# Folding the even channels twice in a Fourier-mixing kernel

## The chip, the cores and the metric

The kernel runs as one program on one core of a Trainium2 chip. The time is device microseconds (us) of an execution; lower is better. Six executions of the kernel before were timed, and one of them was profiled.

## The reference

Two blocks follow each other, all in float32. The first is attention that keeps, for each query, its 32 largest scores; its result, with the heads laid side by side, is `x` of shape (8, 576, 512). The second is a Fourier mixing block with an MLP:

```python
X = np.fft.fft(x, axis=1)          # over 576 tokens
X = np.fft.fft(X, axis=2)          # over 512 channels
u = x + np.real(X)
un = (u - mean(u)) / sqrt(var(u) + 1e-6)
out = u + np.maximum(un @ w_ch1, 0.0) @ w_ch2     # 512 -> 2048 -> 512
```

The change touches only the two Fourier transforms, which are done as matrix products with tables of cosines and sines.

## The kernel before

**Batches and steps.** There are 8 batches of 36 steps (4 pairs of heads by 9 tiles of queries). In each step TensorE computes scores (`sp`, line 360) and transposes an earlier tile's weights (`tpP`, L427), VectorE finds the 32 largest scores with four `MAX8` and three `MATCH_REPLACE8` (L381, L383), GpSimd turns them into bounds (`nt`, L390), ScalarE and GpSimd mask the scores with those bounds (L397, then L400), and ScalarE takes the exponential (L406). When a batch's attention is over, its Fourier transforms come within the first 16 or so steps of the next batch, and its MLP (`hp` L832, `cp` L859, `cw` and `cv` L1029) is cut into units that fill TensorE's free time in the steps that follow. A planner (`plan`, `costs`, `level`, the loop from L1348) assigns every piece to a step at build time from estimated costs. The emitted order is the order in which each engine executes; nothing is reordered at run time between the queues. The planner's estimate for the channel transform is 1.75 us a tile and for the token transform 4.3 us per parity (L1291, L1295).

**The folds.** A transform of real data by cosines and sines needs half the products if entries that mirror each other are added or subtracted first. For each parity `par` of the output token, `fold_ops` (L582) makes four operations: `first` adds or subtracts the two halves of the tokens (`sd`, L602), `second` adds and subtracts the two halves of the channels (`zw`, L565), giving 256 columns for the even output channels and 256 for the odd ones, and two calls of `fold_channels` (L546) fold each of these 256 once more about its middle (`fg`, L549). `fold_tails` does the same for the 64 left-over tokens into `ftail`. The fold operations run on GpSimd for batches 1 to 6, one operation to a step there (batch 1: the last two in one step), and on VectorE for batches 0 and 7, all in a row. On GpSimd they stand in a step behind that step's masking (L400) and ahead of its bounds (L390), so the next step's masking waits for them.

**The token transform.** `half_of_tokens` (L620) takes 128 folded channels as the stationary operand and a table `fs` of 145 columns as the moving one, for three blocks of tokens. Half `g2` = 0 holds the even channels (cosine part and sine part), `g2` = 1 the odd ones. One middle channel of the even half is computed by three products with one stationary column each. ScalarE writes the result `yp` to `y`, twice: as it is, and mirrored (L658 to L660), the mirrored sine part through a multiplication with a sign from `sg`.

**The channel transform.** `dft_channels` (L669) multiplies, for each of a batch's five token tiles, four blocks of `y` (128 channels each) with the table `fd`: two blocks make the 256 even output channels, two the 256 odd ones. Its result `mp` is copied to `us` by ScalarE, interleaved so that even and odd channels alternate (L699), and GpSimd adds it to `x` (L705); in batches 0 and 7 VectorE adds it to `x` directly (L688). Mean and variance (L710), the transpose `tpu` (L747) and the MLP follow.

A float32 product appears in the trace as two passes, so 15 products of the token transform for one parity show as 30 matmul records, and the channel transform of one tile as 8. A transpose is one record.

Of the kernel before, what the change touches and what calls it, by code (L numbers as in the profile page):

```python
# [9 lines left out]
F32 = mybir.dt.float32  # L10
# [3 lines left out]
ALU = mybir.AluOpType  # L14
# [4 lines left out]
P = 128  # L19
# [3 lines left out]
def _tables(S, DM):  # L23

    kq = S // 4 + 1
    p = np.arange(P)
    fs = np.zeros((P, 2, 2, 3, kq), dtype=np.float64)
    for par in range(2):
        kk = 2 * np.arange(kq) + par
        for st in range(3):
            tok = P * st + p
            if st == 2:  # L40

                tok = np.where(p < TH, tok, S // 2 + tok - TH)
            a = 2.0 * np.pi * ((np.outer(tok, kk) % S) / S)
            fs[:, 0, par, st] = np.cos(a)
            fs[:, 1, par, st] = np.sin(a)
    d = np.arange(DM // 4)
    m = np.arange(DM // 2)

    def ang(dd, ll):
        return 2.0 * np.pi * ((np.outer(dd, ll) % DM) / DM)  # L50

    se = -np.sin(ang(d, 2 * m))
    se[0] = np.cos(np.pi * m)
    so = -np.sin(ang(d + 1, 2 * m + 1))
    fd = np.stack([np.cos(ang(d, 2 * m)), se, np.cos(ang(d, 2 * m + 1)), so], axis=1)
    sg = -np.ones((P, 2))
    sg[0, 0] = 1.0
    return (
        fs.astype(np.float32), fd.astype(np.float32), sg.astype(np.float32),
        np.eye(P, dtype=np.float32),  # L60
    )
# [3 lines left out]
def kernel(  # L65
# [9 lines left out]
    nc = tc.nc  # L75
    B, H, S, D = q.shape
    DM = H * D
    DF = moe_w_ch1.shape[1]
    scale = 1.0 / float(D) ** 0.5
    HS = S // 2  # L80
    NC = 5
    NF = NC - 1
    TAIL = 2 * TH
# [44 lines left out]

    ident = const.tile([P, P], F32, name="ident", tag="ident")
    fs = const.tile([P, 2, 2, 3, KQ], F32, name="fs", tag="fs")  # L130
    fd = const.tile([P, 4, DM // 2], F32, name="fd", tag="fd")
    sg = const.tile([P, 2], F32, name="sg", tag="sg")
    w1 = const.tile([P, NDT, DF], F32, name="w1", tag="w1")
    w2 = const.tile([P, NIT, DM], F32, name="w2", tag="w2")
    mv = [const.tile([P, 5, 2], F32, name=f"mv{i}", tag=f"mv{i}") for i in range(2)]
# [401 lines left out]
        return 0.14 * len(CHUNKS[ch])  # L537


    def two(ap):  # L540
        return ap.rearrange("p (m two) -> p two m", two=2)

    Q1, Q2, Q3 = DM // 4, DM // 2, 3 * DM // 4
    folded, y_of, yt_of, us_of, rs_of, unT_of = ({} for _ in range(6))

    def fold_channels(eng, z, f, n):  # L546

        def tt(out, up, down, op):
            eng.tensor_tensor(out=f[..., out], in0=z[..., up], in1=z[..., down], op=op)  # L549

        if n == 0:
            eng.memset(f[..., Q1:Q1 + 1], 0.0)
            eng.tensor_copy(out=f[..., 0:DM:Q2], in_=z[..., 0:DM:Q2])
            up, down = slice(1, Q1), slice(Q2 - 1, Q1, -1)
            tt(up, up, down, ALU.add)
            tt(slice(Q1 + 1, Q2), up, down, ALU.subtract)
        else:
            up, down = slice(Q2 + 1, Q3), slice(DM - 1, Q3, -1)
            tt(up, up, down, ALU.subtract)
            tt(slice(Q3, DM - 1), up, down, ALU.add)  # L560
            eng.tensor_copy(out=f[..., DM - 1:DM], in_=z[..., Q3:Q3 + 1])

    def fold_halves(eng, s_, z):
# [3 lines left out]
    def fold_tails(b, eng):  # L567


        f, got = ftail[0:TAIL], []  # L570

        def first():
            got.append(batp.tile([P, DM], F32, name=f"zt_{b}", tag="fold_s")[0:TAIL])
            fold_halves(eng, x_of[b][0:TAIL, 4, :], got[0])

        def third():
            fold_channels(eng, got[0], f[:, 0:DM], 1)
            eng.tensor_copy(out=f[:, DM:DM + 1], in_=got[0][:, Q1:Q1 + 1])

        return [first, lambda: fold_channels(eng, got[0], f[:, 0:DM], 0), third]  # L580

    def fold_ops(b, par, eng, space="own"):  # L582

        x = x_of[b]

        if space == "hT":
            sp = batp.tile([P, NIT * CW[0]], F32, name=f"fsp_{b}", tag="hT")

        def buf(n, name):
            if space == "hT":
                return sp[:, 2 * DM * n:2 * DM * (n + 1)].rearrange("p (s c) -> p s c", s=2)
            pool, tag = (batp, ("fold_s", "fold_d")) if space == "own" else (attp, ("PT0", "PT1"))
            return pool.tile([P, 2, DM], F32, name=f"{name}_{b}_{par}", tag=tag[n % 2], bufs=1)

        got = folded[b, par] = []

        def first():
            got.append(buf(0, "sd"))  # L600
            op = ALU.add if par == 0 else ALU.subtract
            eng.tensor_tensor(out=got[0], in0=x[:, 0:2, :], in1=x[:, 2:4, :], op=op)  # L602

        def second():
            got.append(buf(1, "zw"))
            fold_halves(eng, got[0], got[1])

        def third(n):
            if n == 0:
                got.append(buf(2, "fg"))  # L610
            fold_channels(eng, got[1], got[2], n)

        return [first, second, lambda: third(0), lambda: third(1)]

    def dft_tokens(b, par):
        for g2 in range(2):
# [3 lines left out]
    def half_of_tokens(b, par, g2):  # L620
# [11 lines left out]
        def mm(gg, st, lhsT, rows, table, start=False):  # L632

            nc.tensor.matmul(  # L634
                yp[0:rows, gg, :],
                lhsT=lhsT,
                rhs=fs[:, table, par, st, :],
                start=start,
                stop=st == 2,
                skip_group_check=True,  # L640
            )


        for gg in range(2):
            g = 2 * g2 + gg
            for st in range(3):
                f = fg[:, st] if st < 2 else ftail
                mm(gg, st, f[:, P * g:P * (g + 1)], P, gg, start=gg == 0 and st == 0)
        if g2 == 0:
            for st in range(3):  # L650
                mm(1, st, zw[:, st, Q1:Q1 + 1] if st < 2 else ftail[:, DM:DM + 1], 1, 0)

        mir, back = (
            (slice(HS + 2, S, 2), slice(KQ - 2, 0, -1)) if par == 0
# [1 line left out]
        )  # L656
        y2 = y[:, 2 * g2:2 * g2 + 2, :]
        nc.scalar.copy(out=y2[:, :, par:HS + 1:2], in_=yp[:, :, 0:KQ - par])  # L658
        nc.scalar.copy(out=y2[:, 0, mir], in_=yp[:, 0, back])
        nc.scalar.mul(out=y2[:, 1, mir], in_=yp[:, 1, back], mul=sg[:, g2:g2 + 1])  # L660
        if par == 1 and g2 == 1:
            tails_of_y(b)

# [5 lines left out]
    def dft_channels(b, t, quick=False):  # L669

        rows, y = ROWS[t], y_of[b]
        shape, name = [P, 2, DM // 2], f"mp_{b}_{t}"
        mp = ps_s.tile(shape, F32, name=name, tag="sp") if b == B - 1 else bank(shape, name)
        for par in range(2):
            for j in range(2):
                g = 2 * par + j
                if t == 4:
                    lhsT = yt_of[b][:, g].rearrange("p h r -> p (h r)")
                else:
                    k0 = HS * (t // 2) + P * (t % 2)  # L680
                    lhsT = y[:, g, k0:k0 + P]
                nc.tensor.matmul(  # L682
                    mp[0:rows, par, :], lhsT=lhsT, rhs=fd[:, g, :],
                    start=(j == 0), stop=(j == 1),
                )
        if quick:
            xt = two(x_of[b][0:rows, t, :])
            at(now[0], "dve", lambda: nc.vector.tensor_tensor(  # L688
                out=xt, in0=mp[0:rows], in1=xt, op=ALU.add
            ))  # L690
# [5 lines left out]
                [P, 2 if key[1] else 3, DM], F32, name=f"us_{b}_{t}", tag="fold_d" if key[1] else "fold_s"  # L696
            )
        us = us_of[key][0:rows, CHUNKS[int(key[1])].index(t), :]
        nc.scalar.copy(out=two(us), in_=mp[0:rows])  # L699
        return 1.75  # L700

    def add_mixed(b, t):
# [802 lines left out]
```

## Time and profile before

| what | value |
|---|---|
| median of 6 runs | 1911.79 us (1910.22 to 1912.96) |
| the profiled execution's own time | 1912.96 us |
| its span, first to last instruction | 1911.2 us |
| TensorE busy | 1796.9 us (94%) |
| VectorE busy | 1583.4 us (83%) |
| ScalarE busy | 1210.3 us (63%) |
| GpSimd busy | 877.2 us (46%) |
| mean granted TensorE clock | 0.974 |
| chain of waits: share on TensorE | 81% |

The engines are named PE (TensorE), PEld (its weight loads), DVE (VectorE), ACT (ScalarE), POOL (GpSimd) and SP (the queue that issues most transfers). The chain of waits follows the work that ended last back from the end: at each step to what released it, or to the instruction before it on its engine. "x8" behind a chain piece counts matmul records. In the lists in order of time, the first number is the start in us and the second the duration of the merged piece; an arrow in brackets names what ended the idle time before it.

### The profile page before, as it was taken

The numbers are of one execution on the slowest core, as the hardware profiler recorded it, in microseconds if no ns is written. First come the engines' busy times: TensorE is split into PE (matmuls) and PEld (weight loads), VectorE is DVE, ScalarE is ACT, GpSimd is POOL, SyncE is SP. The second block draws the span as 40 slices with busy tenths as digits, with TensorE's granted clock in tenths as the row PEclk, the third lists the DMA queues.
The fourth block names the chain that finished last, engine by engine and source line by source line (L and its number), as shares of the span: only waits on it lengthen the run. The fifth ranks groups of instructions, "written<-read, shape, count | busy, mean of one in ns | idle before, by whom it ended". The sixth has DMA issues, their size and how long they took to land.

```text
span 1911.2 us, 28279 instructions
## 1 busy us (share of the span) xinstructions
PE 1796.9 (94%) x9008; PEld 1190.8 (62%) x9008; DVE 1583.4 (83%) x3277; ACT 1210.3 (63%) x3078; POOL 877.2 (46%) x1158
## 2 busy tenths in 40 slices
PE   5567799999999999999999999999999999999999
PEld 3344465474666756766567656667567656667677
DVE  7999989999999999989898898888899888862110
ACT  6878657676766767666676667766676667652100
POOL 4768643555635454345535454355535454341012
PEclk7787899999999999999999999999999999999999
DMA  5333002211104111140013101140013102030132
GB/s 167 103 95 107 20 13 61 88 56 25 47 24 119 31 27 41 42 121 19 19 47 110 46 14 52 42 121 19 19 47 101 52 17 59 23 102 6 50 106 73
DMA packets 184339, 111.34 MB, mean 58 GB/s; under 512 B 125952, under 2 KB 174208, under 8 KB 184192
## 3 DMA queue, kind: packets, MB, share of 16 engines
q1 hardware_dynamic: 183408, 109.33, 20.2%
q8 instruction: 72, 1.18, 0.3%
q14 instruction: 75, 0.61, 0.1%
q10 hardware_dynamic: 784, 0.21, 0.0%
HBM read 93.76 MB, written 15.73 MB: 57 GB/s over the span
## 4 chain that ended last, share of the span: by engine, by line
PE 81%; ACT 7%; DVE 6%; POOL 3%; DMA 2%; issue 1%; SPq 0%; POOLq 0%; DVEq 0%; ACTq 0%
PE hp L832 25%; PE cp L859 11%; PE o L464 8%; PE tpP L427 6%; PE sp L360 6%; PE cw L1029 5%; PE cv L1029 4%; PE yp L634 3%; PE mp L682 3%; PE cp L898 3%; DVE m L381 3%; DVE wk L383 2%; PE sp_t L330 2%; POOL wk L400 1%; ACT wk L406 1%
## 5 line engine op out<-in xcount | busy, mean ns | idle before, releaser
L400 POOL TENSOR_TENSOR wk<-S,wk 128x576 f32<-128x576 f32 x288 | 408.3, 1418 | 771.0 <-ACT wk L397 742.4
L381 DVE MAX8 m<-wk 128x8 f32<-128x576 f32 x864 | 626.5, 749 | 6.1
L832 PE MATMUL hp<-unT,w 128*128 128x256 f32 (+1 forms) x2048 | 538.4, 410 | 2.6 <-ACT unT L750 2.6
L832 PEld LDWEIGHTS hp<-unT,w 128*128 128x128 f32 x2048 | 373.7, 191 | 124.2 <-issue 25.0
L383 DVE MATCH_REPLACE8 wk<-m,wk 128x576 f32<-128x576 f32 x576 | 427.6, 742 | 0.0
L406 ACT ACTIVATE wk<-wk,nt 128x576 f32<-128x576 f32 x288 | 224.9, 781 | 71.6 <-POOL wk L400 67.5
L427 PE MATMUL tpP<-ident,wk 128*128 128x128 f32 x1152 | 183.1, 283 | 70.8 <-ACT wk L406 43.1
L430 ACT COPY PT<-tpP 128x512 f32<-128x512 f32 (+1 forms) x320 | 171.4, 547 | 111.9 <-PE tpP L427 109.6
L859 PE MATMUL cp<-w,hT 128*128 128x512 f32 x512 | 240.6, 598 | 0.0
L397 ACT ACTIVATE wk<-S,nt 128x576 f32<-128x576 f32 x288 | 226.9, 788 | 19.4 <-POOL nt L390 18.4
L427 PEld LDWEIGHTS tpP<-ident,wk 128*128 128x128 f32 x1152 | 140.7, 145 | 143.6 <-ACT wk L406 66.2
L836 ACT ACTIVATE hT<-hp 128x320 f32<-128x320 f32 (+1 forms) x256 | 104.9, 410 | 193.6 <-PE hp L832 191.5
L381 DVE MAX8 m<-S 128x8 f32<-128x576 f32 x288 | 213.8, 743 | 5.3 <-ACT S L334 5.3
L383 DVE MATCH_REPLACE8 wk<-m,S 128x576 f32<-128x576 f32 x288 | 213.7, 742 | 0.0
L464 PE MATMUL o<-PT,v 128*64 128x256 f32 (+3 forms) x1440 | 193.4, 411 | 1.7 <-ACT PT L430 1.7
L363 ACT COPY S<-sp 128x512 f32<-128x512 f32 (+1 forms) x264 | 141.9, 589 | 51.7 <-PE sp L360 51.5
L360 PE MATMUL sp<-kT,qT 64*128 64x512 f32 (+1 forms) x528 | 159.0, 661 | 4.3 <-ACT means L1217 3.3
L464 PEld LDWEIGHTS o<-PT,v 128*64 128x64 f32 x1440 | 110.5, 151 | 73.1 <-issue 15.7
L859 PEld LDWEIGHTS cp<-w,hT 128*128 128x128 f32 x512 | 88.8, 190 | 86.3 <-issue 86.2
L974 POOL TENSOR_TENSOR hT<-hT 128x512 f32<-128x512 f32 x64 | 81.5, 1276 | 101.0 <-ACT hT L836 89.3
L1029 PE MATMUL cw<-w,hT 128*128 128x256 f32 x448 | 106.8, 383 | 2.7 <-DMA w<-w_parts 1.3
L1029 PEld LDWEIGHTS cw<-w,hT 128*128 128x128 f32 x448 | 81.4, 190 | 20.4 <-issue 6.4
(143 smaller groups left out, 2149.0 us busy)
## 6 DMA issues: line engine op xcount, KB each, us to landing
w<-w_parts SPq DMA_DIRECT2D x82, 512.0 KB, 4.4
space<-in_moe_w_ch_dram SPq DMA_DIRECT2D x32, 512.0 KB, 3.6
nat<-in_q_dram SPq DMA_DIRECT2D x128, 64.0 KB, 2.3
v<-in_v_dram SPq DMA_DIRECT2D x128, 64.0 KB, 2.2
out_dram<-x SPq DMA_DIRECT2D x32, 256.0 KB, 2.1
nat<-in_k_dram SPq DMA_DIRECT2D x124, 64.0 KB, 2.2
w_parts<-w_t SPq DMA_DIRECT2D x8, 512.0 KB, 2.9
w_s<-w_parts SPq DMA_DIRECT2D x8, 512.0 KB, 5.0
```

Of the source, the lines that this page charges most:

```text
L360: nc.tensor.matmul(sp[r], lhsT=qT[hd, q_cols], rhs=kT[hd, :], start=True, stop=True)
L381: ops.append(lambda src=src, m8=m8: nc.vector.max(out=m8, in_=src))
L383: ops.append(lambda src=src, m8=m8: nc.vector.match_replace(w, m8, src, NEG))
L397: nc.scalar.activation(out=w, in_=Ssb[i], func=AF.Relu, scale=-FAR, bias=Nt[i][:, 1:2])
L400: nc.gpsimd.tensor_tensor(out=w, in0=Ssb.pop(i), in1=w, op=ALU.subtract)
L406: nc.scalar.activation(out=w, in_=w, func=AF.Exp, bias=Nt.pop(i)[:, 0:1], accum_out=den_t[pair % 3][:, c:c + 1],)
L427: nc.tensor.transpose(tp[:, c, :], p_sb[:, k0 + P * c:k0 + P * (c + 1)], ident)
L430: nc.scalar.copy(out=pt[:, NF * he:NF * (he + 1), col:col + w], in_=tp[:, :, o:o + w])
L464: nc.tensor.matmul(o[D * e:D * (e + 1), c0:c1], lhsT=vv[:, c, e, :], rhs=pt[:, 2 * NF if c == NF else NF * e + c, c0:c1], start=(c == 0), ...
L832: nc.tensor.matmul(hp[:, 0:w], lhsT=w1[:, dt, P * it:P * (it + 1)], rhs=unT[:, dt, 0:w], start=(dt == 0), stop=(dt == NDT - 1),)
L859: nc.tensor.matmul(cp, lhsT=hT[:, it, P * n:P * (n + 1)], rhs=w2[:, it, :], start=(it == 0), stop=(it == NIT - 1),)
L1029: nc.tensor.matmul(dst, lhsT=h()[a][:, kc, :], rhs=rhs_of(kc), start=start and kc == 0, stop=kc == NK - 1, skip_group_check=True,)
```

## The change

The even half of the channels is folded once more. After the first fold of the 256 even columns into 128 sums and 128 differences (now kept in 256 extra columns `c` behind `fg`), each of these 128 is folded about its own middle into 64 cosine and 64 sine columns. `fold_channels` now has three parts: part 0 the first even fold (into `c`), part 1 the second even fold (four additions or subtractions of 63 or 64 columns, one zeroed column, one copied column), part 2 the odd fold with one more copied column. In `fold_ops` parts 0 and 1 form the third operation of the four, part 2 the fourth; in `fold_tails` part 0 joins the first operation, part 1 is the second, part 2 the third.

In the token transform the even half's two groups of 128 channels now each hold 64 cosine and 64 sine columns. Each is done as two products with 64 stationary columns, one into result rows 0 to 63 with the cosine table and one into rows 64 to 127 with the sine table, alternating: 12 products in place of 6 per parity. The three products with one column remain, with row 64 of the first group as their result. The mirrored copy of the first even group becomes a multiplication by a sign (64 rows of each), where it was a plain copy.

In the channel transform the even half becomes two independent products of 128 moving columns, one for the output channels that are a multiple of four and one for those two beyond, in place of two accumulated products of 256 columns. The odd half keeps its two products of 256 columns, with its table's columns in another order. The result now holds four groups of 128, and `us` and the addition to `x` interleave with a step of four elements in place of two.

The costs and steps in the planner stay as they were.

```diff
-    def fold_channels(eng, z, f, n):
+    def fold_channels(eng, z, f, c, n):
         if n == 0:
-            eng.memset(f[..., Q1:Q1 + 1], 0.0)
-            eng.tensor_copy(out=f[..., 0:DM:Q2], in_=z[..., 0:DM:Q2])
+            eng.tensor_copy(out=c[..., 0:Q1 + 1:Q1], in_=z[..., 0:Q1 + 1:Q1])
             up, down = slice(1, Q1), slice(Q2 - 1, Q1, -1)
-            tt(up, up, down, ALU.add)
-            tt(slice(Q1 + 1, Q2), up, down, ALU.subtract)
+            tt(c, up, z, up, down, ALU.add)
+            tt(c, slice(Q1 + 1, Q2), z, up, down, ALU.subtract)
+        elif n == 1:
+            up, down = slice(0, Q0), slice(Q1, Q0, -1)
+            tt(f, slice(0, Q0), c, up, down, ALU.add)
+            tt(f, slice(Q1, Q1 + Q0), c, up, down, ALU.subtract)
+            up, down = slice(Q1 + 1, Q1 + Q0), slice(Q2 - 1, Q1 + Q0, -1)
+            tt(f, slice(Q0 + 1, Q1), c, up, down, ALU.subtract)
+            tt(f, slice(Q1 + Q0 + 1, Q2), c, up, down, ALU.add)
+            eng.memset(f[..., Q0:Q0 + 1], 0.0)
+            eng.tensor_copy(out=f[..., Q1 + Q0:Q1 + Q0 + 1], in_=c[..., Q1 + Q0:Q1 + Q0 + 1])
         else:
...
+            eng.tensor_copy(out=f[..., Q2:Q2 + 1], in_=z[..., Q2:Q2 + 1])
             eng.tensor_copy(out=f[..., DM - 1:DM], in_=z[..., Q3:Q3 + 1])
...
-        return [first, second, lambda: third(0), lambda: third(1)]
+        def both():
+            third(0)
+            third(1)
+
+        return [first, second, both, lambda: third(2)]
...
                 f = fg[:, st] if st < 2 else ftail
-                mm(gg, st, f[:, P * g:P * (g + 1)], P, gg, start=gg == 0 and st == 0)
+                first = gg == 0 and st == 0
+                if g2:
+                    mm(gg, st, f[:, P * g:P * (g + 1)], slice(0, P), gg, first)
+                    continue
+                for h in range(2):
+                    c0 = P * g + P // 2 * h
+                    mm(gg, st, f[:, c0:c0 + P // 2], slice(P // 2 * h, P // 2 * (h + 1)), h, first)
         if g2 == 0:
             for st in range(3):
-                mm(1, st, zw[:, st, Q1:Q1 + 1] if st < 2 else ftail[:, DM:DM + 1], 1, 0)
+                f, c = (fg[:, st], DM + Q0) if st < 2 else (ftail, DM)
+                mm(0, st, f[:, c:c + 1], slice(Q0, Q0 + 1), 0)
...
-        nc.scalar.copy(out=y2[:, 0, mir], in_=yp[:, 0, back])
-        nc.scalar.mul(out=y2[:, 1, mir], in_=yp[:, 1, back], mul=sg[:, g2:g2 + 1])
+        if g2:
+            nc.scalar.copy(out=y2[:, 0, mir], in_=yp[:, 0, back])
+        else:
+            nc.scalar.mul(out=y2[:, 0, mir], in_=yp[:, 0, back], mul=sg[:, 0:1])
+        nc.scalar.mul(out=y2[:, 1, mir], in_=yp[:, 1, back], mul=sg[:, 1 + g2:2 + g2])
...
-        for par in range(2):
-            for j in range(2):
-                g = 2 * par + j
...
-                nc.tensor.matmul(
-                    mp[0:rows, par, :], lhsT=lhsT, rhs=fd[:, g, :],
-                    start=(j == 0), stop=(j == 1),
-                )
+        for g in range(2):
+            nc.tensor.matmul(mp[0:rows, 0, g, :], lhsT=of(g), rhs=fd[:, g], start=True, stop=True)
+        for g in range(2, 4):
+            nc.tensor.matmul(
+                mp[0:rows, 1], lhsT=of(g), rhs=fd[:, 2 * g - 2:2 * g],
+                start=(g == 2), stop=(g == 3),
+            )
...
-        nc.scalar.copy(out=two(us), in_=mp[0:rows])
+        nc.scalar.copy(out=four(us), in_=mp[0:rows])
```

## Prediction

> **What bounds the kernel now.** I read the busy times first, then the chain of waits, then the chain near one batch's transforms, then the lists in order of time around the folds. The page, first and fourth part:
>
> ```profile
> PE 1796.9 (94%) x9008; PEld 1190.8 (62%) x9008; DVE 1583.4 (83%) x3277; ACT 1210.3 (63%) x3078; POOL 877.2 (46%) x1158
> ...
> PE 81%; ACT 7%; DVE 6%; POOL 3%; DMA 2%; issue 1%; SPq 0%; POOLq 0%; DVEq 0%; ACTq 0%
> ```
>
> TensorE carries the chain. How tightly is read from the busy times of one batch's period in mid-kernel (length; PE, PEld, DVE, ACT and POOL busy; granted clock):
>
> ```profile
> 1326.50:1542.80 216.30, 215.15 (x1107) 143.02 (x1105) 192.28 (x398) 145.17 (x372) 99.17 (x137) 1.00 0.19 52
> ```
>
> TensorE idles for 1.15 us of 216.3, so in batches 3 to 6 what TensorE saves is mostly time, if no other engine holds it up. The chain near batch 6's transforms gives the price of each product (start, length, records):
>
> ```profile
> 1505.81 1.06 PE sp L360 x4
> ...
> 1513.90 1.73 PE hp L832 x8
> ...
> 1541.75 1.06 PE sp L360 x4
> 1542.81 4.20 PE yp L634 x30
> ...
> 1562.33 2.31 PE o L464 x20
> ...
> 1577.60 0.22 PE sp_t L330 x2
> 1577.82 0.55 PE tpk L274 x5
> 1578.37 1.72 PE cp L859 x4
> 1580.09 4.00 PE yp L634 x30
> 1584.09 0.44 PE tpP L427 x4
> 1584.53 0.11 PE tpP_t L438
> 1584.63 1.06 PE sp L360 x4
> 1585.69 3.65 PE mp L682 x16
> ```
>
> `hp` has 256 moving columns here: 1.73 / 8 = 0.216 us a pass. `sp_t` has 128 stationary and 128 moving columns: 0.110. `o` has 64 stationary columns, in two column halves that alternate, and 256 moving columns: 20 passes in 2.31, 0.115 each, so two halves take the time of one whole. The token transform (`yp`) takes 4.00 behind whole-array work and 4.20 behind `sp`, which uses half the rows: entering or leaving a divided array costs 0.15 to 0.2.
>
> **The change part by part.** The profiled execution took 1912.96 us, 1.8 beyond its span of 1911.2 and 1.2 above the median of 1911.79; I sum differences and set them against the median. Below 0.2% (3.8 us) a measurement of this kernel can't tell a difference from none.
>
> *Channel transform.* Each of 40 tiles swaps four passes at 0.216 for four at 0.110: 4 x 0.106 = 0.42 us, 2.12 a batch, 17.0 in all. The 128 x 128 weight load is the danger at 128 moving columns, but `sp_t` has both and holds 0.110.
>
> *Token transform.* Twelve whole passes per parity become 24 half passes, with 145 moving columns. By `o` a pair costs one whole pass, so nothing is added for the passes. In the first batch 18 of its half passes with 128 columns took 1.31 us including a last record of 0.27, or 0.061 each; a half pass here may take 0.0625 (whole passes start 0.125 apart), so the weight loads just keep up. The array is divided earlier: where `yp` follows whole-array work (parity 1 of eight batches, parity 0 of the last), entering adds 0.15, from `o`: 2.31 less ten whole passes at 0.216. Nine times, +1.4; behind `sp` it was paid already. Bounds: 0 and 16 x 0.2 = 3.2; I take 1.4 because the rows differ exactly there. The Trainium skill speaks against this part: its page TensorEngine Tiling (Array Packing), Key Properties, says that a change of tiling mode drains the array. A full drain of one pass (0.285 us by the `yp` records) at all 16 places would make it 4.6 instead of 1.4; the step from 4.00 to 4.20 is smaller, and I go by it. TensorE in all: 17.0 - 1.4 = 15.6 saved, if every microsecond counts.
>
> *Folds on GpSimd* (batches 1 to 6). The rows (duration ns min/median/max):
>
> ```profile
> L549 POOL TENSOR_TENSOR fg<-zw x48: 714/728/741, 467.9 to 1569.5; 128x254 f32<-128x254 f32 x48
> L549 POOL TENSOR_TENSOR ftail<-zt x32: 445/448/455, 225.1 to 1725.8; 64x127 f32<-64x127 f32 x32
> ```
>
> Time goes with the elements: the four new operations have 126 or 128, so 0.45 each, 0.415 back to back (two of the tail took 0.86). Third operation: +1.66 and a copy of 0.15, fourth +0.15: +2.0 per parity. Tails +1.5 a batch (four at 0.30, extra copies). In all +36 us on 877. Behind a fold on its queue stand `nt`, then ScalarE's masking in order, then L400 and the exponential. In batches 3 to 6 the slack covers it: at parity 0 of batch 6 the fold would end at 1537.9, 0.8 late for the masking at 1537.05, but ScalarE then idles 1.0 and 1.57 us; at parity 1 the masking (1565.30) slips by 1.9 and the exponential of 1569.60 still finds its data, while TensorE's transposes at 1573.57 come 3 us later. Both transforms start two or more steps after the folds. Cost taken: 0 on the path, 10 x 2.0 = 20 if nothing covered it.
>
> *Batch 1* has no such steps. In order of time:
>
> ```profile
> 467.93 2.79 POOL L549 TENSOR_TENSOR fg<-zw 128x254 f32<-128x254 f32 x4
> ...
> 469.38 0.55 PEld L634 LDWEIGHTS yp<-fs,fg 128*128 128x128 f32 x4 [0.76 <-POOL fg L549]
> ...
> 485.43 0.54 PEld L634 LDWEIGHTS yp<-fs,fg 128*128 128x128 f32 x4 [0.63 <-POOL fg L549]
> ```
>
> The transform starts as soon as its first columns exist, 0.97 us after the fold's begin at parity 1. Now its second product needs the zeroed column, behind both even folds: 0.15 + 1.40 + 1.66 + 0.05 = 3.25. So +2.3 at parity 1; at parity 0, 467.74 + 3.25 = 471.0 against 469.4, +1.6. The chain runs through both. Batch 1: 1.6 + 2.3 + 0.15 - 2.12 = +1.9.
>
> *Folds on VectorE.* By its rows (0.416 for 254 elements, 0.688 for 512) 128 elements take 0.28, 0.22 back to back; with copies +1.1 per parity. Batch 7: parity 0's fold ends at 1747.8 and its transform starts at 1749.73; parity 1's at 1751.8 and 1758.88, so slack covers 1.1 and 2.3, TensorE working on `cp`. Its value is 0.3 - 2.12 = -1.8. Batch 0: the parity 1 transform starts at 239.13 straight behind VectorE's fold, and would now start at about 241.5; with 2.1 returned by the channel transform the PE path is +0.4, VectorE's own queue +2.3. VectorE is busy 39.0 of the next 44 us. I take +1.0 of 0.4 to 2.5.
>
> *Batches 2 to 6.* Full value 2.12 - 0.15 = 1.97 each. But after each token transform VectorE, which waited 5.0 us for a transpose, works without a gap through the channel steps (its statistics add 4.3 us there); TensorE's lead over it there is about 2 us, which the change uses up. Batch 2's chain passes through VectorE from 719 to 747, so I take 0.7 of its 1.97 and 80% for the other four: 6.3.
>
> *ScalarE.* Sixteen mirrored copies at 0.295 become multiplications at 0.408: 1.8 us, hidden since the next half's products run meanwhile (uncovered: 1.8). The interleaved write goes from a step of 8 bytes to 16. No row has 16. The 8-byte copies (632 ns) are 7% above plain ones of the same size (589); VectorE's (692) equal plain additions (688). Bounds: 0, and a doubling: 0.63 us once in each of batches 1 to 6 where the last tile's copy is on the path (at 1600.21), and five of 0.69 in batch 0: 7. I take 0, nearest to the 8-byte rows. The Trainium skill, page SBUF — State Buffer, section SBUF: two separate sides, says that 16-byte lines run at full bandwidth with at least two hits per line; a 16-byte step has one. It gives no price; by the doubling the sum would be 7 higher. No row here shows it.
>
> Transfers and queues: SP gets nothing, the constant table shrinks.
>
> Sum: batch 0 +1.0, batch 1 +1.9, batch 2 -0.7, batches 3 to 6 -6.3, batch 7 -1.8: **-5.9 us**, 1911.8 - 5.9 = 1905.9.
>
> **The rivals.**
>
> *GpSimd's long folds reach the path in batches 2 to 6 (slower).* For: in batch 2 at 701 and batch 1 GpSimd already paces the masking (gaps of 0.89, ScalarE's latency). Against: the slack in batches 3 to 6. Each of 10 folds can cost up to 2.0; at 0.97 each it cancels the gain to slower by 0.2% (5.9 + 3.8 = 9.7). At 1.3 each: 1905.9 + 13 = 1919.
>
> *The two column halves run one after the other (slower).* Against: `o`. Price: 16 x 12 half passes, each taking a whole 0.125: 24 us, 1930; it decides from 40% of that.
>
> *VectorE becomes the bound in the channel steps (same).* For: its gapless stretch, batch 2. Against: 24 us of idle time per period elsewhere. With a third of the gain in batches 2 to 6: -1.8 + 2.9 - 3.3 = -2.2, 1909.6. The costlier interleaved write ends near here too: -5.9 + 4 = -2, 1910.
>
> **How the numbers follow.** Main case 0.53, with its own range 1901 to 1908 (full value in batches 2 to 6 and half of batch 1's loss: -10.7; half of it lost: -3.5). VectorE or write 0.27, 1908 to 1913. GpSimd 0.15, 1914 to 1925; halves 0.05. Faster 0.54, same 0.26, slower 0.20. Leaving out the lowest 0.08 and the highest 0.12: 1899 to 1917.
>
> **What would show it.** Right: `mp` x16 near 2.8 us in the chain; `yp` near 4.15 to 4.2 at both parities with 42 products; GpSimd near 913 us; batch 1's transform idling before `yp` for GpSimd; periods of mid-kernel near 214.7. Wrong: `yp` over 5 us (halves serial); TensorE waiting for the exponential behind the folds; L699 near 1 us; VectorE's waits for TensorE gone and the period unchanged.

## The result, and the profile after

The changed kernel takes 1917.68 us (median of 19 runs, 1914.09 to 1920.14), the kernel before in the same series 1912.38 us (39 runs, 1908.78 to 1913.67). The ratio is 1.0030, with a 95% interval of 1.0024 to 1.0036: 0.3%, or 5.7 us by the ratio (5.3 by the medians), slower, where 5.9 us faster were predicted. The profiled execution of the changed kernel took 1915.88 us with a span of 1914.1; it lies 1.8 us below its median, as the one of before lay 1.2 us above its own, so that the two traces show 2.9 us of the difference.

The page of the changed kernel, first part, and the row for one mid-kernel period (length; PE, PEld, DVE, ACT, POOL busy; granted clock; DMA):

```profile
PE 1791.3 (94%) x9200; PEld 1181.5 (62%) x9200; DVE 1588.4 (83%) x3301; ACT 1221.6 (64%) x3078; POOL 910.4 (48%) x1278
...
1117.00:1332.70 215.70, 213.36 (x1130) 141.11 (x1130) 192.06 (x398) 147.43 (x372) 104.20 (x155) 1.00 0.19 52
```

TensorE's work in that period fell from 215.15 to 213.36 us, by 1.79, but the period fell from 216.3 to 215.7 only: TensorE now idles 2.34 us in it, where it idled 1.15. Two thirds of the saving went into waiting. The chain of waits behind a parity 1 transform in mid-kernel, which in the kernel before ran through the channel products, tells for what:

```profile
1154.22 4.17 PE yp L662 x42
1158.41 0.42 ACT y L693
...
1162.78 1.95 ACT us L738 x2
...
1167.78 1.94 ACT us L738 x2
...
1173.38 1.08 ACT us L738
1174.60 0.64 PE tpu L786 x4
```

From 1158.41 to 1174.60, for 16.2 us, ScalarE works almost without a gap and sets the pace. Of its work there, five copies of the channel transform are longer than they were, and so are VectorE's additions in batches 0 and 7. The groups of instructions (duration in ns, minimum/median/maximum), before and changed:

```profile
L699 ACT COPY us<-mp x30: 605/632/651, 494.6 to 1600.2; 128x512 f32<-128x512 f32 x24, 64x512 f32<-64x512 f32 x6
L688 DVE TENSOR_TENSOR x<-mp,x x10: 684/692/693, 245.2 to 1773.8; 128x512 f32<-128x512 f32 x8, 64x512 f32<-64x512 f32 x2
...
L738 ACT COPY us<-mp x30: 1068/1116/1205, 499.6 to 1604.8; 128x512 f32<-128x512 f32 x24, 64x512 f32<-64x512 f32 x6
L727 DVE TENSOR_TENSOR x<-mp,x x10: 1030/1060/1082, 244.7 to 1778.9; 128x512 f32<-128x512 f32 x8, 64x512 f32<-64x512 f32 x2
```

This is the write with a step of 16 bytes; the addition also reads `x` with that step. The second place is batch 1. TensorE's instructions in order of time, with the idle time before them in brackets:

```profile
467.84 0.46 PE L662 MATMUL yp<-fs,fg 128*64 128x145 f32 x2 [0.32 <-POOL fg L558]
469.12 0.59 PE L662 MATMUL yp<-fs,fg 128*64 128x145 f32 x5 [0.82 <-POOL fg L572]
...
487.65 0.46 PE L662 MATMUL yp<-fs,fg 128*64 128x145 f32 x2 [1.44 <-POOL fg L558]
488.93 0.58 PE L662 MATMUL yp<-fs,fg 128*64 128x145 f32 x5 [0.82 <-POOL fg L572]
```

These are the waits that were predicted, 1.1 and 2.3 us long, of which 0.4 at the second transform was there before. What was not predicted: behind each, TensorE is slow. The windows around them (the figure behind the POOL column is the granted clock, 1.00 in both before), and pieces of the chain, two of before and two of the changed kernel:

```profile
475.00:482.00 7.00, 5.62 (x28) 2.72 (x28) 4.73 (x10) 4.32 (x13) 4.77 (x6) 0.76 0.01 2
...
489.00:496.00 7.00, 7.00 (x54) 5.10 (x55) 6.93 (x15) 3.56 (x11) 3.32 (x8) 0.76 0.62 193
```

```profile
477.36 2.87 PE o L464 x20
485.44 4.27 PE yp L634 x30
...
477.49 3.89 PE o L471 x20
...
488.93 5.81 PE yp L662 x40
```

The attention products took 2.87 us before, the transform 4.27. Taking the starts of the parity 0 transforms as marks gives a table of where the time lies in the profiled executions (us; the last three columns are kernels of the experiments). Where batch 1 is folded twice, its mark lies behind both waits of the parity 0 transform, 1.3 us after that transform's first product (467.84 in the changed kernel), so the first wait stands in the row above batch 1's:

| stretch | before | changed | 8-byte write | and batch 1 folded once | and idle time filled |
|---|---|---|---|---|---|
| until batch 1's transform | 469.45 | 469.12 | 469.67 | 468.70 | 469.13 |
| batch 1 to 2 | 211.47 | 218.47 | 216.40 | 211.44 | 211.30 |
| batch 2 to 3 | 213.09 | 213.72 | 213.41 | 214.80 | 213.14 |
| from batch 3 to 6, each of the three | 216.27 | 215.72 | 214.81 | 214.81 | 214.83 |
| batch 6 to 7 | 207.08 | 206.47 | 205.23 | 205.36 | 205.60 |
| from batch 7's on | 161.31 | 159.15 | 158.35 | 158.78 | 158.63 |
| span | 1911.2 | 1914.1 | 1907.5 | 1903.5 | 1902.3 |

### The profile page after: what moved, and what is told of

Read it like the earlier page. It is cut to its first block, busy times and chain, and to the rows that moved or that the text cites. A ratio compares the mean times of both kernels' runs of the same rounds, so it can differ in the third digit from the quotient of the medians.

```text
span 1914.1 us, 28799 instructions
## 1 busy us (share of the span) xinstructions
PE 1791.3 (94%) x9200; PEld 1181.5 (62%) x9200; DVE 1588.4 (83%) x3301; ACT 1221.6 (64%) x3078; POOL 910.4 (48%) x1278
## 4 chain that ended last, share of the span: by engine, by line
PE 76%; DVE 9%; ACT 8%; POOL 3%; issue 2%; DMA 1%; SPq 0%; POOLq 0%; DVEq 0%; ACTq 0%
PE hp L871 26%; PE cp L898 10%; PE o L471 7%; PE tpP L434 5%; PE sp L367 5%; PE cw L1068 5%; PE cv L1068 4%; DVE m L388 4%; PE yp L662 3%; DVE wk L390 3%; PE cp L937 3%; PE sp_t L337 2%; ACT wk L413 1%; POOL wk L407 1%; ACT us L738 1%
```

## The experiments

Times of the kernel before move by a microsecond or two between series, so each kernel is compared by its ratio to the runs of before of the same series.

**The write, undone in two ways.** The first kernel reads PSUM in turns and so writes with a step of 8 bytes again:

```diff
-        return ap.rearrange("p (m b a) -> p a b m", b=2, a=2)
+        return ap.rearrange("p (m b a) -> p a m b", b=2, a=2)
...
-        nc.scalar.copy(out=four(us), in_=mp[0:rows])
+        nc.scalar.copy(out=four(us), in_=mp[0:rows].rearrange("p a b m -> p a m b"))
```

> The changed kernel, with ScalarE's copy of a channel product and VectorE's quick addition writing by 8-byte steps again: the two even products are read from PSUM in turns (one element of each), where the changed kernel reads them one after the other and writes by 16-byte steps. Theory W (the 16-byte-step write, 0.48 us more for each of five copies, lies on the path of batches 1 to 6 because ScalarE, with TensorE's channel work shorter, ends last there): the copy falls from 1.12 to 0.65 us, ScalarE's runs in the chain behind the parity-1 transforms go, the periods of batches 3 to 6 fall from 215.7 to 214.0, and the kernel takes 1908 to 1911 us, 7 to 10 less than the changed kernel, the batch-0 additions (five of 0.36 less) among it. Rival G (GpSimd's longer folds, on the path in batches 2 to 6, ate the gain): the copy is shorter but the periods stay within 0.3 us of 215.7; 1915 to 1918. Rival R (it is the access pattern as a whole, not the side it lies on, that costs): the copy stays above 1 us and nothing changes.

Measured: 1909.33 us, ratio 0.9995 (0.9986 to 1.0004), 0.35% or 6.7 us below the changed kernel. The copies, and TensorE's period:

```profile
L738 ACT COPY us<-mp x30: 614/632/672, 500.3 to 1599.5; 128x512 f32<-128x512 f32 x24, 64x512 f32<-64x512 f32 x6
```

```profile
1114.30:1329.00 214.70, 213.29 (x1129) 141.09 (x1130) 192.06 (x398) 145.53 (x372) 104.08 (x155) 1.00 0.19 52
```

Reading 128 elements apart costs nothing; writing 16 bytes apart does. The period falls by 0.9 to 214.8, 1.46 below before: three quarters of the 1.97 that the prediction had as full value, where it had taken 80%. Theory W holds for the write; its figure of 214.0 a period was too low, since the next engine takes over. The chain behind the parity 1 transform now runs through VectorE, for 22 us from 1156.25 on:

```profile
1160.70 1.46 DVE wk L390 x2
1162.16 1.34 DVE m L388 x2
...
1164.34 0.61 DVE st L749
```

The second kernel lets TensorE interleave:

```diff
-            nc.tensor.matmul(mp[0:rows, 0, g, :], lhsT=of(g), rhs=fd[:, g], start=True, stop=True)
+            nc.tensor.matmul(
+                mp[0:rows, 0, g:DM // 2:2], lhsT=of(g), rhs=fd[:, g], start=True, stop=True
+            )
```

> The changed kernel, with the two even products of the channel transform writing every second PSUM column each, so that ScalarE and VectorE read in order and write by 8-byte steps as in the kernel before; the odd table columns are in natural order again. The interleaving is thereby moved to TensorE's output. Theory W: the copy takes 0.63 us as before, the periods of batches 3 to 6 fall from 215.7 to 214.0, and the kernel takes 1907 to 1911 us if a 128-column pass keeps its 0.11 us with a stepped output. If the stepped output costs TensorE as much as it saved (0.22 a pass), the kernel loses 2.1 us a batch against that and takes about 1922 to 1926. Rival G (GpSimd's folds): within 2 us of the changed kernel, 1915 to 1918, with short copies.

Measured: 1910.19 us, ratio 0.9993 (0.9984 to 1.0001). A product of 128 columns takes 275 ns (median), stepped output or not, the copy 630 ns. The two ways give the same time, and what they have in common, the 8-byte write, is the cause.

**The write alone, in the kernel before.**

```diff
+    fd = np.concatenate([fd[:, :, 0::2], fd[:, :, 1::2]], axis=2)
...
-        return ap.rearrange("p (m two) -> p two m", two=2)
+        return ap.rearrange("p (m b a) -> p a b m", b=2, a=2)
...
-        nc.scalar.copy(out=two(us), in_=mp[0:rows])
+        nc.scalar.copy(out=two(us), in_=mp[0:rows].rearrange("p a (b m) -> p a b m", b=2))
```

The second pair of lines gives `two` the body of the changed kernel's `four`, with its step of 16 bytes.

> The kernel before with one thing of the change alone: the table columns of the channel transform reordered so that ScalarE's copies and VectorE's quick additions write by 16-byte steps. Same products, same folds. Theory W, for the price: ScalarE's copy goes from 0.63 to 1.12 us and the addition from 0.69 to 1.06; on the path, since TensorE with its 1.75 us a tile is still the longer one behind most transforms (ScalarE busy 16.7 of 19.5 us there), only part of 5 x 0.48 = 2.4 us a batch: 0.5 to 1.5 in each of batches 1 to 6 and 1 to 2 in batch 0, 1916 to 1921 us in all (4 to 9 more than before). Rival H (the write is covered by other work wherever it lies, and what was lost was lost to the folds or the divided array): within 2 us of before, 1910 to 1914.

Measured: 1913.9 us, ratio 1.0012 (1.0003 to 1.0021), 2.3 us more than before, between what Theory W (4 to 9) and Rival H (within 2) had expected; the copy has the changed kernel's 1116 ns. Batch 1's period grows by 0.9, each of batches 3 to 5 by 0.46. The same instructions, longer by the same 0.48 us, cost half as much in mid-kernel as with the shorter products (0.9). The write and the saving meet in one stretch: what shortened TensorE's channel work is what put ScalarE's copies on the path.

**More work for TensorE ahead of batch 1's transforms.**

```diff
+            at(T0 + 4, "pe1", lambda: one_unit() if len(queue) > 1 else 0.0)
+            at(T0 + 7, "pe1", lambda: one_unit() + one_unit() if len(queue) > 2 else 0.0)
```

> The changed kernel, with three units of TensorE work that wait in the queue of batch 0's MLP put ahead of batch 1's two token transforms (one ahead of the first, two ahead of the second), where TensorE idles for GpSimd's folds. Theory F (batch 1 lost 7.0 us, of it about 3.5 in the two waits for the folds and the rest in the drop of the granted clock to 0.76 that follows them): the waits of 5.2 and 4.4 us for the folds shrink to under 2 us in sum, the granted clock stays at 1.00 from 470 to 520 us, batch 1's period falls from 218.5 to 212 to 214 and the kernel takes 1912 to 1915 us. Rival P (the MLP units are wanted later as cover for other waits of batch 1 or 2, so that the idle time only moves): batches 1 and 2 together stay within 1.5 us of 432.2 and the kernel within 2 us of 1917.7. Rival C (the clock falls for a reason other than the idle time): the waits go and the windows near 475 and 490 us still show 0.76; then batch 1 falls by 3 us only.

Measured: 1916.32 us, ratio 1.0028 (1.0017 to 1.0040). The experiment failed: the queue of batch 0's MLP holds too little in those steps for the edit's conditions, so every engine has as many instructions as in the changed kernel. It tells that hardly any useful work is at hand there, and is a second measurement of the changed kernel.

**Needless work there instead**, on the kernel that reads in turns:

```diff
+        for _ in range(12 if b == 1 and g2 == 0 else 0):
+            nc.tensor.matmul(
+                yp[:, 0, :], lhsT=ident, rhs=fs[:, 0, par, 0, :], start=True, stop=True,
+                skip_group_check=True,
+            )
```

> The kernel that reads PSUM in turns (the changed kernel with the 8-byte write), with 12 needless products of 145 columns, about 1.5 us of TensorE work whose result is overwritten, ahead of each of batch 1's two token transforms, where TensorE waits 1.7 and 2.3 us for GpSimd's folds. Nothing is left out. Theory I (the drop of the granted clock to 0.76 at 475 to 482 and 489 to 496 us follows from the idle time added there): the waits are filled, the clock stays at 1.00 in both windows, the second transform takes 4.2 instead of 5.8 us and the attention products 2.9 instead of 4.1 us; batch 1's period falls from 216.4 to 213 to 214 and the kernel takes 1906 to 1908 us. Rival C (the clock falls for another reason, or the added products do not count): the windows still show 0.76 and the period stays at 216 to 217; 1909 to 1911.

Measured: 1908.9 us, ratio 0.9994 (0.9985 to 1.0003): no gain in the time. The windows and the chain:

```profile
475.00:482.00 7.00, 4.72 (x36) 3.52 (x35) 4.16 (x10) 5.35 (x17) 3.81 (x4) 1.00 0.01 4
...
489.00:496.00 7.00, 7.00 (x70) 6.08 (x72) 6.93 (x14) 2.68 (x8) 5.51 (x14) 1.00 0.60 172
```

```profile
480.71 2.84 PE o L471 x20
...
488.40 2.96 PE yp L673 x24
491.36 4.17 PE yp L662 x42
```

The clock stays at 1.00 in both windows and the products behind the waits have their old durations (2.84 and 4.17 us). With the added idle time filled, the falls are gone: Theory I's mechanism. The added idle time is not all of it. Every trace with batch 1's old steps has the wait of 2.28 us ahead of the attention products. Behind it they are slow in all five traces that have the added waits (3.89 to 4.38 us), and at their 2.87 in six of the seven traces whose batch 1 is folded once; the seventh follows below. Theory I's time was mis-sized: a product is two records of 0.13 us, so twelve took 3.0 to 3.2 us and not 1.5, more than the waits that they cover, and pushed the transforms back by about what the clock gave.

**The folds spread over more steps**, again with reading in turns:

```diff
-                        at(T0 + 1 + 3 * par + min(n, 2), "pool0", op)
+                        at(T0 + 1 + 4 * par + n, "pool0", op)
...
-            ft, fc = (T0 + 4, T0 + 7), T0 + 8
+            ft, fc = (T0 + 5, T0 + 9), T0 + 10
```

> The kernel that reads PSUM in turns, with batch 1's folds on GpSimd one operation in each step instead of the third and the fourth in the same step, and the transforms one and two steps later, the form that the other batches have. Theory F (batch 1's loss of 5.0 us lies in TensorE waiting for the folds in those steps, and the clock that falls behind it): the waits for the folds shrink from 3.4 us to under 1 us, the clock stays at 1.00, and batch 1's period falls from 216.4 to 212 to 214; 1905 to 1907 us. Rival D (batch 0's MLP is done by then, so that TensorE has nothing else to do; two steps more until the channel transform only move the idle time, and batch 1's MLP comes later): the period stays at 216 to 221, 1909 to 1914.

Measured: 1910.0 us, ratio 1.0001 (0.9993 to 1.0010). Rival D: TensorE no longer waits for the folds, but 2.1 us each for ScalarE's copies of the next pair's transposed keys and queries, and the clock falls there too (0.79 from 489 to 496 us); batch 2's transform starts at 686.35, against 686.07 without the spread, and batch 6's period, under the moved plan, is 208.5 instead of 205.2.

**Batch 1 folded once.** `ONCE` is the batch whose even half keeps the form of the kernel before; its table is brought in as batch 0's MLP leaves its space:

```diff
+    ONCE = (1,)
...
+        if b in ONCE and n == 0:
+            eng.memset(f[..., Q1:Q1 + 1], 0.0)
+            eng.tensor_copy(out=f[..., 0:1], in_=z[..., 0:1])
...
+        elif b in ONCE and n == 1:
+            pass
...
+            if b in ONCE:
+                nc.tensor.matmul(
+                    mp[0:rows, 0], lhsT=of(g), rhs=fe_of[0][:, 2 * g:2 * g + 2],
+                    start=(g == 0), stop=(g == 1),
+                )
```

> The kernel that reads PSUM in turns, with the change undone in batch 1 alone: its even channels are folded once, its token transform uses whole products and its channel transform two products of 256 columns for the even half, from a table of its own that is brought in for the batch (256 KB by SP's queue, into space that batch 0's MLP has left). Theory F (the second fold is what makes batch 1 longer): batch 1's period returns to between 211.0 and 212.5 us, the waits for GpSimd's folds to 0.4 us, the clock to 1.00; the kernel takes 1904 to 1906 us, 4 to 5 less than with the change in batch 1, and 5 to 7 less than before. Rival E (batch 1's loss comes from elsewhere: batch 0's shorter work that moves the transform against VectorE's steps): the period stays above 215, 1908 to 1911.

Measured: 1904.66 us, ratio 0.9973 (0.9961 to 0.9984): 0.22% or 4.2 us below the kernel that reads in turns, and 0.27% faster than before. Batch 1's period is the old one, 211.44, and its waits for the folds are the old 0.4 us. Not foreseen: batch 2 takes 1.4 us more. There TensorE waits 3.3 us for VectorE to free a bank of PSUM, and the clock falls:

```profile
740.00:745.00 5.00, 3.66 (x9) 2.64 (x10) 4.83 (x15) 1.06 (x2) 1.57 (x8) 0.55 0.70 212
```

The clock is 0.76 in the next 5 us. The wait itself is not new: the kernel that reads in turns has it as well (3.24 us, with a clock of 0.67 from 745 to 750). The MLP's products behind it take 3.39 us there and 4.47 here, which is 1.1 of the 1.4 us; in each kernel this is one execution.

**The changed kernel with batch 1 folded once**, its 16-byte write kept: the same edit on the changed kernel.

> The changed kernel, its 16-byte-step write kept, with the change undone in batch 1 alone, as in the kernel that gained 4 to 5 us by it. Theory W+F (the two losses, the write and batch 1's second fold, lie in different places and add up): 4 to 5.5 us less than the changed kernel, 1911 to 1914 us, equal to the kernel before within 0.15%; mid-kernel periods stay at 215.7 and batch 1's falls from 218.5 to between 211.5 and 213. Rival (they overlap, the write's share of batch 1 being part of the same wait): 1914 to 1917.

Measured: 1910.22 us, ratio 0.9997 (0.9989 to 1.0006), 6.3 us below the changed kernel. Either one undone brings the kernel back to before. The mid-kernel periods stay at 215.7, but batch 1's falls to 213.9 only, where 211.5 to 213 was expected. No new wait stands there (0.38 us for the folds, as before), and still the clock falls behind the old wait of 2.28 us:

```profile
475.00:482.00 7.00, 6.66 (x29) 2.90 (x30) 5.50 (x13) 4.00 (x13) 4.02 (x4) 0.76 0.00 0
...
476.00 4.56 PE o L476 x20
```

By the ratios the two causes are worth 6.7 and 6.3 us alone and 6.7 + 4.2 = 10.9 together. That is 2.1 less than the sum, which is not clear of noise: each ratio is uncertain by about 0.1%, or 2 us. By the spans it is 6.6, 5.5 and 10.6, and the periods say where the 1.5 us lie. Batch 1 gains 2.1 by the write, 4.6 by the single fold and 7.0 by both, so there the two add up; batch 2 gains 0.3 and 0.2, but loses 1.1 when both are undone.

**GpSimd's folds in batches 3 to 6.** With reading in turns, the second even fold is done twice:

```diff
-            third(1)
+            for _ in range(2 if 3 <= b <= 6 else 1):
+                third(1)
```

> The kernel that reads PSUM in turns, with the second even fold done twice on GpSimd in batches 3 to 6 (the same values written again): GpSimd's queue gets some 1.8 us more per parity, eight times, about as much as the change itself had added. Theory W (GpSimd's longer folds are off the path in batches 3 to 6): their periods stay at 214.8 within 0.3 us and the kernel takes 1908 to 1911 us. Rival G (GpSimd's folds cost time there): each doubling costs 0.5 to 1.8 us on the path, periods of 216 to 218.4 and 1914 to 1924 us.

Measured: 1910.92 us, ratio 1.0003 (0.9994 to 1.0012). GpSimd is busy 923.9 us instead of 908.9: eight times 1.87. From batch 3's transform to batch 7's it is 851.0 us, against 849.7: 1.3 us for 15 us of added work. Of these, 1.1 lie in batch 3, where TensorE now waits 0.9 us for the exponential and the chain ahead of that runs through the doubled folds. Rival G is out for the change itself in batches 3 to 6, but its mechanism exists: at twice the added work the slack is used up at one place.

**The idle time of batch 2.** Three runs on the one transposition that waits for a bank. The first, on the kernel with batch 1 folded once, puts needless products into that wait:

```diff
+        if (pair, ch) == (13, 0):
+            spare = ps_t.tile([P, KQ], F32, name="spare", tag="tp")
+            for _ in range(9):
+                nc.tensor.matmul(spare, lhsT=ident, rhs=fs[:, 0, 0, 0, :], start=True, stop=True)
```

> The kernel with the 8-byte write and batch 1 folded once, with nine needless products of 145 columns (18 records of 0.13 us, 2.4 us) ahead of the one transposition in batch 2 for which TensorE waits 3.3 us until VectorE has read the bank that it writes. Nothing is left out and nothing useful is added. Theory I (the granted clock, 0.55 and 0.76 from 740 to 750 us, falls because of that idle time): the clock stays at 1.00 there, the products behind it take 2.2 instead of 4.5 us, batch 2's period falls from 214.8 to 212 to 213, and the kernel takes 1902.0 to 1903.5 us, 1.5 to 2.5 less than without them: work that is not needed makes it faster. Rival C (the clock falls for another reason): the products fill the wait and the clock still falls; 1904 to 1906.

Measured: 1903.66 us, ratio 0.9963 (0.9950 to 0.9975).

```profile
738.31 2.49 PE L518 MATMUL spare<-fs,ident 128*128 128x145 f32 x18
741.63 0.55 PE L520 MATMUL tpx<-ident,xT 128*128 128x128 f32 x3 [0.84 <-DVE x L524]
742.02 2.32 PE L908 MATMUL hp<-unT,w 128*128 128x320 f32 x8
```

```profile
740.00:745.00 5.00, 4.16 (x26) 3.26 (x25) 4.83 (x14) 1.96 (x5) 1.46 (x8) 1.00 0.66 206
```

The transposition starts when VectorE lets it, as before, but the clock is 1.00 and the products behind it take 2.32 us, where the trace without the filling has 4.47. Batch 2's period falls by 1.66 to 213.14. The gain in time is not shown: the ratios of the two kernels differ by 0.1%, their intervals overlap, and part of the 1.66 can be the execution, since the same wait cost 3.39 us of products in another trace. This is the fastest kernel of the study, 0.37% below before. The second and the third run give the transposition another bank, in that kernel (without the filling) and in the kernel before:

```diff
-        tp = ps_o.tile(shape, F32, name=name, tag="o") if at_once else bank(shape, name)
+        own = at_once and (pair, ch) != (13, 0)
+        tp = ps_o.tile(shape, F32, name=name, tag="o") if own else bank(shape, name)
```

> The kernel with the 8-byte write and batch 1 folded once, where that same transposition of batch 2 writes another PSUM bank, one of the three that the MLP rotates through, so that TensorE doesn't wait there for VectorE. Theory V (TensorE's saving in batch 2 was lost only to this wait for VectorE, and to the clock behind it; after 760 us TensorE is busy without a gap, so what is not lost there is won): the wait of 3.3 us goes, the clock stays at 1.00, batch 2's period falls from 214.8 to 209.5 to 211, and the kernel takes 1899 to 1901 us. Rival D (VectorE sets batch 2's pace, and the wait returns at the next product that needs its work, its statistics or a bank): the period falls by less than 2 us, 1902.5 to 1905.

> The kernel before, with the one transposition of batch 2 moved to another PSUM bank and nothing else, so that the gain of the same edit on the kernel with the change can be told from the change's own. TensorE waits 1.15 us there, with no drop of the clock behind it. Theory V: the kernel takes 0.5 to 1.2 us less than before, below what can be told: 1909.5 to 1912. Rival: more than 2 us less, 1909 or below: then the edit is worth as much without the change.

Measured: 1908.85 us, ratio 0.9991 (0.9982 to 1.0000), and 1914.07 us, ratio 1.0020 (1.0011 to 1.0029): both slower than the kernel they are built on, by 3.4 us in batch 2's period each. The transposition starts at once, and the bank that it takes is then missing to the MLP:

```profile
748.64 4.61 PE L905 MATMUL hp<-unT,w 128*128 128x320 f32 x8 [6.42 <-DVE x L528]
```

A wait of 3.3 us became one of 6.4, with a clock of 0.50 to 0.54 around it (in the kernel before, 1.15 became 4.3, with 0.66 over 5 us), since VectorE, which carries the chain there with `MAX8` and its replacements until 748, reads that tile no sooner. VectorE sets batch 2's pace: Rival D, and worse.

## Why the prediction was wrong

*What bounds the kernel* was read rightly for TensorE, but the reading "what TensorE saves is mostly time" holds only as far as the next engine: ScalarE, and behind it VectorE, were within 1 to 2 us of it in the stretch that the change shortens (an estimate from the 1.2 of 1.8 us that became waiting in a period).

*Channel transform*, 0.42 us a tile: right. The four passes of 128 columns take 0.45 and the other four 0.87, together 0.41 less than the 1.73 of before.

*Token transform*: right. `yp` takes 4.15 to 4.17 at both parities with 42 records (4.15 to 4.20 predicted), so the column halves run side by side. The rival of serial halves is out.

*Folds on GpSimd*: right in size (910.4 us against 913) and in effect: even doubled they cost 1.3 us in all in batches 3 to 6, and in batch 2 no wait of TensorE is for a fold, nor is one in the chain. The rival of long folds on the path in batches 2 to 6 is out.

*ScalarE*: **the failed step is "I take 0, nearest to the 8-byte rows" for the interleaved write.** Both bounds were given, 0 and a doubling of 0.63 us. The chip gave 1.12 us for the copy, 0.48 more, and 1.06 for VectorE's addition, 0.37 more: three quarters of a doubling for the one, half for the other. And the place was counted too small: one copy per batch was said to lie on the path; in the trace of after the chain goes through all five, 2.4 us more a batch, of which 0.9 came through to a mid-kernel period. The upper bound of 7 us for the whole is almost the 6.7 that undoing it brought. The 8-byte rows were the nearest rows, but they stood on the near side of a step, and nearness says nothing across one. The rule of the Trainium skill that was set against the row (SBUF — State Buffer, section SBUF: two separate sides, with its two hits per 16-byte line) pointed the right way (484 ns more a copy); its example of four fp32 values as a free step does not agree with these 1116 ns.

*Batch 1*, +1.9 predicted, of which 1.6 lie ahead of the table's mark; its period grew by 7.0. Up to batch 2's mark, +2.9 were predicted for batches 0 and 1 together, and the traces give +6.7 (+5.2 with the 8-byte write). The waits were near (1.6 and 2.3 more predicted, 1.1 and 1.9 more measured). Two things were not in the sum. The clock that falls behind them cost about 3 us: 1.0 on `o`, 0.45 on the transposes ahead of it, 1.55 on `yp`. And the 2.12 that the channel transform was to give back did not come back: with the 8-byte write the second transform ends 25.8 us behind the start of the first, where it was 20.3 before (1.9 more of waiting, about 3 by the clock), and the period is still 4.9 longer, so that only 0.6 was regained. The first product of the first transform did start 1.5 earlier than before (467.84 against 469.38), but the waits there took that.

*Batch 2*, -0.7 predicted, +0.6 measured, +0.3 without the write: VectorE set the pace there as the trace of before had shown, TensorE's saving became waiting, and the clock fell behind the waiting as well.

*Batches 3 to 6*, -6.3 predicted: the periods of the changed kernel give 3 x 0.55 + 0.61 = -2.3, those with the 8-byte write 3 x 1.46 + 1.85 = -6.2. The mechanism and its discount of 20% were right; the write took the rest. *Batch 7* gave -2.2, and -3.0 with the 8-byte write, against -1.8; that stretch differs by 1.1 us between two executions of the same instructions (161.3 in the kernel before, 160.2 in its variant with the moved transposition). *Batch 0*: the +1.0 is not to be seen; the start of batch 1's transform differs by 2.2 us between these two (469.45 and 467.29).

Put together with the measured terms: -5.9, plus 6.6 for the write (by the spans), plus 3.0 for batch 1 (4.9 in place of 1.9), plus 1.0 for batch 2 (+0.3 in place of -0.7), less 1.2 and 0.8 for batches 7 and 0, makes +2.7, near the 2.9 of the two traces. Of these corrections only the write and batch 1 are clear of what moves between executions. By the traces the kernel with the 8-byte write takes 3.7 us less than before, by the ratio 1.0 (0.9986 to 1.0004): without the write the change comes out at about the time of before, not 5.9 us below it. In the prediction's own range the lower end, -10.7, leaves out batch 0's +1.0: by its terms it is -9.7. The write stood among the rivals with +4, together with VectorE as the bound, as a case of no change; it came with more, and together with batch 1's loss.

## What to carry to other kernels

Before you shorten one engine's part in a stretch, add up the busy time of the other engines in that same stretch: the saving ends at the next of them, and from there on what the change adds to that one is paid as well (here the added 2.4 us a batch cost 0.9 with the shorter products and 0.46 without). An operand pattern that no row shows, here a step one power of two wider, is an unknown price: time it alone before the change is built, or choose a form that has a row, here by moving the interleaving to the side where it is free. When you price a new wait of TensorE, allow for the clock behind it: in batch 1 the slow products cost about as much as the added waits, 3 us each.

## What the chip showed that was not expected

- A write of float32 with a step of 16 bytes costs ScalarE 1116 ns for 128x512 where a step of 8 takes 632. VectorE's addition, which reads `x` with the same step as it writes, takes 1060 instead of 692. Reading from PSUM in turns, 512 bytes apart, and writing to PSUM with a step of 8 bytes from TensorE (275 ns either way) cost nothing.
- The granted clock can fall after short idle times: 0.76 over 7 us behind a wait of 2.3 us, 0.55 over 5 us around one of 3.3 us, 0.50 to 0.54 over 10 us around one of 6.4. Needless products in the wait kept it at 1.00, in one trace at each of two places. It does not depend on the wait alone. Behind batch 1's old wait of 2.28 us it fell in all five traces where a new wait of 1.1 us ended 5 us ahead of it, and in one of seven without; at the second new wait, of 2.3 us, it fell in four of the five. The exception is the kernel with the doubled folds, whose batch 1 is that of the kernel that reads in turns: its second transform took 4.23 us instead of 5.81, and batch 1's period was 214.7 instead of 216.4. What decides it in one execution is open.
- The Trainium skill, TensorE: Matmul & The Clock Gate, Part 1: The HAM clock gate, describes a clock that halves after an idle window of about 3.4 us, in windows that run on regardless of the program. That the clock falls in some executions and not in others at the same place fits such windows, though no run here tests it; the wait of 2.28 us, behind which it fell here, is shorter than the window.
